# A fixed step order, DMA transposes and casting weight loads for linear attention followed by an MLP

## The chip, the cores and the metric

The kernel runs on one core of one Trainium2 chip. The metric is the device time of one execution in microseconds, as a median of runs. The profile is one execution taken by the hardware profiler; its span is 1.7 to 2.2 us shorter than the time in the runs that have both on record. A run that is over 1.5% above the fastest of its kernel counts as slow; ratios use fast runs alone.

Names of engines in the views: PE is TensorE (matmuls), PEld its weight loads, DVE is VectorE, ACT is ScalarE, POOL is GpSimd, SPq the queue from which the sync engine issues transfers. PEclk is the TensorE clock that was granted, 1.00 being full speed.

## The reference

```python
# q, k, v: (8 batches, 8 heads, 576 tokens, 64), float32
q_s = softmax(q, axis=-1);  k_s = softmax(k, axis=2)          # k over the tokens
kv  = einsum('bhsd,bhse->bhde', k_s, v)
att = einsum('bhsd,bhde->bhse', q_s, kv)
x   = att.transpose(0, 2, 1, 3).reshape(8, 576, 512)
mu, var = mean and variance of x over its 512 columns
xn  = (x - mu) / sqrt(var + 1e-6) * g_ln
out = x + relu(xn @ w_ch1) @ w_ch2                            # 512 x 2048, 2048 x 512
```

There are 8 x 576 = 4608 tokens, that is nine chunks of 512. The MLP takes 128 matmuls of 512 columns for each chunk: 64 `ph` (16 blocks of hidden columns x 4 blocks of input) and 64 `pc` (4 tiles of tokens x 16 blocks of hidden columns), 1152 in all. In both kernels `rstd` is applied after the second matmul, as relu lets it through.

## The kernel before

It is written for a framework whose scheduler orders the instructions of each engine. Chunks of 512 tokens run across batch borders, so the tiles of a batch are cut unevenly. The parts that matter here:

```python
def attn_load(b):                      # per tile of 128 (or 64) tokens
    nc.sync.dma_start(kt[:sz], k[b, :, s0:s0+sz, :].transpose([1, 0, 2]))   # rows of 256 B
    nc.scalar.activation(ek_b[:sz, st], kt[:sz], AF.Exp)
    ...                                # v: load, copy on ScalarE; q: load, exp on ScalarE
    nc.vector.reduce_sum(zq[:sz], eq[:sz], axis=AX.X)
    nc.vector.reciprocal(rq[:sz], zq[:sz])
    nc.vector.tensor_mul(qs_b[:sz, st], eq[:sz], rq[:sz].to_broadcast([sz, H, D]))

def attn_te(b):
    ...                                # pkv: 64 x 65 per head, 5 matmuls each; kv_b = pkv / sum
    nc.tensor.transpose(ptr[:, j, :], qs_b[:, st, 2*j:2*j+2, :], ident)     # q on TensorE
    nc.vector.tensor_copy(out=qsT_b[:, :, s0:s0+sz], in_=ptr[:, :, :sz])
    ...                                # po = qsT x kv_b
    nc.scalar.copy(x_sb[ro:ro+sz, xt, :], po[ro:ro+sz, :])
    nc.vector.bn_stats(stat_all[ro:ro+sz, xt, :], x_sb[ro:ro+sz, xt, :])

def mlp_prep(ci):
    ...                                # bn_aggr
    nc.scalar.activation(lnv, mv[:, :, 1], AF.Ln, bias=eps_ln)      # one table set
    nc.scalar.activation(rstd, lnv, AF.Exp, scale=-0.5)             # another one
    ...
    nc.tensor.transpose(pxt[:, c, :], xn[:, c*P:(c+1)*P], ident)    # xn on TensorE
    nc.vector.tensor_copy(out=xnT[:, :, ti*P:(ti+1)*P], in_=pxt)

def load_w1():                         # 4 pieces through two staging buffers
    nc.sync.dma_start(wt, w1_src[:, ko, :])
    nc.vector.tensor_scalar_mul(w1_sb[:, ko, :], in0=wt, scalar1=g_sb[:, ko:ko+1])

for b in range(1, B):
    mlp_prep(b - 1)
    if b + 1 < B: attn_load(b + 1)
    attn_te(b)
    mlp_mm(b - 1)
```

The softmax here doesn't subtract the row's maximum and nothing guards it: scores larger than these inputs give would overflow.

## Time and profile before

| | before |
|---|---|
| time, median of 3 runs | 372.78 us (370.8 to 373.81) |
| span of the profiled run | 369.5 us |
| TensorE, VectorE, ScalarE busy | 307.5, 180.3, 184.4 us |
| mean granted TensorE clock | 0.968 |

The page gives busy times, slices and the chain of work that ended last; the prediction below shows those lines and reads them. One more passage of the chain, in order of time (start, length, what), shows what a stall in the middle looks like:

```profile
203.53 0.62 ACT eq L137
204.15 0.49 ACT hT L247
...
204.66 1.28 ACT L218
...
206.27 1.28 ACT L219
...
207.77 0.52 ACT ek_ab L128
208.28 0.49 ACT hT L247
...
208.82 1.03 PE ph L237 x4
```

`L218` and `L219` without a tile are loads of activation tables: `Ln` and `Exp` lie in different sets, so ScalarE changes tables twice in each chunk. The relu `hT` stands behind them, and TensorE, with two PSUM buffers for `ph`, stands behind the relu.

### The profile page before, as it was taken

How to read it: one execution, taken by the hardware profiler on the slowest of the kernel's cores; microseconds unless marked ns; L12 is line 12 of the kernel's file. 1: busy time of each engine (PE TensorE's matmuls, PEld its weight loads, DVE VectorE, ACT ScalarE, POOL GpSimd, SP SyncE). 2: the span in 40 equal slices, each digit the busy share in tenths (PEclk: the TensorE clock that was granted, in tenths of full speed). 3: DMA queues.
4: the chain of work that ended last, by engine and by line, in shares of the span. 5: the costliest groups of instructions: out<-in, count | busy, mean ns of one | idle time of the engine just before them, and what ended most of it. 6: DMA issues, size and time to landing. Idle time of an engine off the chain costs nothing.

```text
span 369.5 us, 4982 instructions
## 1 busy us (share of the span) xinstructions
PE 307.5 (83%) x1904; PEld 152.3 (41%) x1936; DVE 180.3 (49%) x403; ACT 184.4 (50%) x321; POOL 0.7 (0%) x6
## 2 busy tenths in 40 slices
PE   0254795889999879997999799879987989997995
PEld 0142243435444534463455345534443443443442
DVE  4577346855584864694459336921370131122021
ACT  4553485635795498178628853672066104402600
POOL 0000000000000000000000000000000000000000
PEclk9999697799999999999999899999999998999999
DMA  9967992799099497399289618500100020011002
GB/s 179 204 242 261 200 254 113 219 240 228 11 224 245 122 227 123 92 220 215 59 205 209 101 36 219 117 2 25 60 30 1 29 86 0 2 57 57 0 30 85
DMA packets 120984, 46.46 MB, mean 126 GB/s; under 512 B 113793, under 2 KB 113793, under 8 KB 120449
## 3 DMA queue, kind: packets, MB, share of 16 engines
q1 hardware_dynamic: 120960, 46.15, 56.7%
q8 instruction: 15, 0.25, 0.3%
q14 instruction: 9, 0.07, 0.1%
HBM read 36.70 MB, written 9.44 MB: 125 GB/s over the span
## 4 chain that ended last, share of the span: by engine, by line
PE 67%; DVE 13%; ACT 9%; DMA 5%; SPq 3%; issue 2%; ACTq 0%; DVEq 0%
PE pc L253 32%; PE ph L237 29%; DMA qt<-in_q_dram 3%; DVE xnT L228 2%; ACT hT L247 2%; ACT x_sb L200 2%; PE ptr L180 2%; DMA wt<-in_moe_w_ch_dram 2%; ACT L219 2%; DVE stat_all L201 2%; DVE zq L139 2%; PE pkv L159 2%; DVE ot L261 2%; PE po L193 1%; SPq L131 1%
## 5 line engine op out<-in xcount | busy, mean ns | idle before, releaser
L237 PE MATMUL ph<-xnT,w_sb 128*128 128x512 bf16 x556 | 139.4, 393 | 18.3 <-ACT hT L247 11.3
L253 PE MATMUL pc<-w_sb,hT 128*128 128x512 bf16 x564 | 129.1, 382 | 2.7 <-DVE w_sb L117 1.8
L247 ACT ACTIVATE hT<-ph 128x512 bf16<-128x512 f32 x126 | 74.4, 597 | 82.4 <-PE ph L237 81.7
L237 PEld LDWEIGHTS <-w_sb 128*128 128x128 bf16 x576 | 56.0, 100 | 84.5 <-issue 26.6
L253 PEld LDWEIGHTS <-hT 128*128 128x128 bf16 x576 | 56.6, 98 | 69.8 <-issue 3.7
L261 DVE SCALAR_TENSOR_TENSOR ot<-pc,rstd,x_sb 128x512 f32<-128x512 f32 x36 | 26.9, 746 | 58.2 <-PE pc L253 58.1
L245 DVE TENSOR_SCALAR hT<-ph 128x512 bf16<-128x512 f32 x18 | 12.4, 688 | 64.8 <-PE ph L237 64.8
L139 DVE TENSOR_REDUCE zq<-eq 128x8 f32<-128x512 bf16 (+1 forms) x40 | 27.1, 677 | 29.1 <-ACT eq L137 29.1
L128 ACT ACTIVATE ek_ab<-kt 128x512 bf16<-128x512 f32 (+1 forms) x40 | 25.1, 626 | 23.5 <-DMA kt<-in_k_dram 23.5
L200 ACT CAST x_sb<-po 128x512 bf16<-128x512 f32 (+1 forms) x40 | 21.8, 588 | 29.3 <-PE po L193 28.8
L132 ACT CAST v_ab<-vt 128x512 bf16<-128x512 f32 (+1 forms) x40 | 24.8, 621 | 19.8 <-DMA vt<-in_v_dram 19.8
L137 ACT ACTIVATE eq<-qt 128x512 bf16<-128x512 f32 (+1 forms) x40 | 25.2, 631 | 8.8 <-DMA qt<-in_q_dram 8.8
L180 PE MATMUL ptr<-ident,qs_ab 128*128 128x128 bf16 x160 | 16.7, 234 | 14.8 <-DVE qs_ab L142 13.2
L142 DVE TENSOR_TENSOR qs_ab<-eq,rq 128x512 bf16<-128x512 bf16 (+1 forms) x40 | 27.4, 686 | 0.9
L201 DVE BATCH_NORM_STATS2 stat_all<-x_sb 128x6 f32<-128x512 bf16 (+1 forms) x40 | 25.5, 679 | 1.8 <-ACT x_sb L200 1.6
L180 PEld LDWEIGHTS <-qs_ab 128*128 128x128 bf16 x160 | 11.9, 104 | 23.2 <-DVE qs_ab L142 17.7
L227 PE MATMUL pxt<-ident,xn 128*128 128x128 bf16 x144 | 13.0, 230 | 10.1 <-DVE xn L224 10.1
L193 PE MATMUL po<-kv_ab,qsT_ab 128*128 128x128 bf16 (+1 forms) x160 | 16.0, 242 | 6.1 <-DVE kv_ab L172 3.6
L185 DVE COPY qsT_ab<-ptr 128x512 bf16<-128x512 bf16 (+1 forms) x40 | 15.1, 392 | 9.8 <-PE ptr L180 9.3
L228 DVE COPY xnT<-pxt 128x512 bf16<-128x512 bf16 x36 | 13.8, 414 | 11.0 <-PE pxt L227 10.8
L159 PE MATMUL pkv<-v_ab,ek_ab 128*64 128x65 bf16 x320 | 11.4, 209 | 6.3 <-ACT v_ab L132 5.9
L193 PEld LDWEIGHTS <-qsT_ab 128*128 128x128 bf16 (+1 forms) x160 | 11.8, 111 | 10.6 <-issue 5.4
(33 smaller groups left out, 89.4 us busy)
## 6 DMA issues: line engine op xcount, KB each, us to landing
out_dram<-ot SPq DMA_DIRECT2D x36, 256.0 KB, 2.1
kt<-in_k_dram SPq DMA_DIRECT2D x32, 256.0 KB, 5.0
vt<-in_v_dram SPq DMA_DIRECT2D x32, 256.0 KB, 5.0
qt<-in_q_dram SPq DMA_DIRECT2D x32, 256.0 KB, 4.8
wt<-in_moe_w_ch_dram SPq DMA_DIRECT2D x4, 1024.0 KB, 6.0
kt<-in_k_dram SPq DMA_DIRECT2D x8, 128.0 KB, 4.8
vt<-in_v_dram SPq DMA_DIRECT2D x8, 128.0 KB, 4.6
qt<-in_q_dram SPq DMA_DIRECT2D x8, 128.0 KB, 4.4
```

What stands on the lines that cost most here:

```text
L128: nc.scalar.activation(ek_b[:sz, st], kt[:sz], AF.Exp)
L137: nc.scalar.activation(eq[:sz], qt[:sz], AF.Exp)
L139: nc.vector.reduce_sum(zq[:sz], eq[:sz], axis=AX.X)
L142: nc.vector.tensor_mul(qs_b[:sz, st], eq[:sz], rq[:sz].to_broadcast([sz, H, D]))
L180: nc.tensor.transpose(ptr[:, j, :], qs_b[:, st, 2 * j : 2 * j + 2, :], ident,)
L193: nc.tensor.matmul(po[ro : ro + sz, j * 128 : j * 128 + 128], qsT_b[:, j, s0 : s0 + sz], kv_b[:, j, :], start=True, stop=True,)
L200: nc.scalar.copy(x_sb[ro : ro + sz, xt, :], po[ro : ro + sz, :])
L201: nc.vector.bn_stats(stat_all[ro : ro + sz, xt, :], x_sb[ro : ro + sz, xt, :])
L237: nc.tensor.matmul(ph, w1_sb[:, ko, m * P : (m + 1) * P], xnT[:, ko, :], start=(ko == 0), stop=(ko == KO1 - 1),)
L247: nc.scalar.activation(hT[:, m, :], ph, AF.Relu)
L253: nc.tensor.matmul(pc, hT[:, ko2, ti * P : (ti + 1) * P], w2_sb[:, ko2, :], start=(ko2 == 0), stop=(ko2 == KO2 - 1),)
L261: nc.vector.scalar_tensor_tensor(ot, in0=pc, scalar=rstd[:, ti : ti + 1], in1=x_sb[:, xt, :], op0=ALU.mult, op1=ALU.add,)
```

## The change

It rewrites nearly the whole kernel with six intentions. The diff below is shortened. The order of all engines is fixed in the source: each chunk is a list of 128 MLP matmuls ("steps"), and the attention of a later batch is put between them at chosen steps. A chunk is the first 512 tokens of one batch; the last 64 tokens of all batches make the ninth chunk. A token's place is chosen so that loads have rows of 1 KB. `eq` and `xn` are transposed by DMA, except for the first two batches. Weights are cast to bf16 by the DMA, from GpSimd's queue. One table set with both functions is loaded once.

```diff
-    def load_w1():
-        for ko in range(KO1):
-            wt = wload.tile([P, DH], FP32, tag="wtmp")
-            nc.sync.dma_start(wt, w1_src[:, ko, :])
-            nc.vector.tensor_scalar_mul(...)
+    def load_w1(nb):
+        nc.gpsimd.dma_start(w1_sb[:, :, cols], w1_src[:, :, cols])   # float32 -> bf16
+    def main_src(x, b, h0, hn):
+        return x[b, h0 : h0 + hn, 0:SM, :].rearrange("h (p t) d -> p h (t d)", t=T)
 ... (kv for two heads at once, 128 x 129) ...
+    def dma_T(dst, src, t0, tn):
+        nc.sync.dma_start_transpose(dst[:, t0:t0+tn].rearrange("p t j c -> p (t j) c"), src)
+    def po_mm(c, t, i):
 ...
+        else:                                  # ninth chunk: two batches in one tile
+            ps = slice(64 * (i // NP), 64 * (i // NP) + 64)
+            nc.tensor.matmul(po[ps, j*P : j*P+P], eqTs[c][:, t, j, ps],
+                             kv_sb[:, 2*t + i // NP, j, :], start=True, stop=True)
+    def x_out(c, t):                           # q's normalisation when po is taken out
+        nc.vector.tensor_mul(x[:, t], pobox["p"], eqs[c][2][:, t].to_broadcast([P, H, D]))
+        stats(c, t, x[:, t])                   # bn_stats, bn_aggr, xn = (x - mean) * g
+    def run(main, side): ...                   # side work at its step between main's matmuls
+    def attn_side(c, kv0, kv1, po0, po1, pe=False):
 ...
+        else:
+            s.append(((po0 + po1) / 2 + 12, lambda: xn_T(c, 0, 2)))
+            s.append((po1 + 12, lambda: xn_T(c, 2, 2)))
+    def first_batch():
+        nc.scalar.preload_act_table_set("natural_log_exp_and_others")
 ...
+        nc.gpsimd.tensor_copy(out=gate, in_=raws[0][0][:, 5, 0, 0:4])   # weights wait for k
+        for nb in range(4): load_w1(nb)
 ...
-    for b in range(1, B):
-        mlp_prep(b - 1) ...
+    with tc.manual_schedule(engines={PE, DVE, Activation, SP, Pool}):
+        first_batch()
+        run(mlp_steps(0), [(60, lambda: load_batch(2))] + prep_side(1, 74, 104, True)
+                          + attn_side(1, 96, 108, 109, 123, True))
+        for c in range(1, B):
+            if c == 1: side += prep_side(2, 0, 30)
+            if c + 1 < B: side += attn_side(c + 1, 34, 54, 62, 90)
+            else:         side += attn_side(C9, 0, 0, 40, 80)
+            if c + 2 < B:
+                side += [(1, lambda b=c + 2: load_batch(b))]
+                side += prep_side(c + 2, 70, 118)
 ...
+            run(mlp_steps(c), side)
+        run(mlp_steps(C9), [])
```

## The prediction

> **What bounds the kernel now.** I read the page first: shares, slices, then the chain of work that ended last.
>
> ```profile
> PE 307.5 (83%) x1904; PEld 152.3 (41%) x1936; DVE 180.3 (49%) x403; ACT 184.4 (50%) x321; POOL 0.7 (0%) x6
> PE   0254795889999879997999799879987989997995
> PEclk9999697799999999999999899999999998999999
> PE 67%; DVE 13%; ACT 9%; DMA 5%; SPq 3%; issue 2%; ACTq 0%; DVEq 0%
> ```
>
> TensorE is the busiest engine and 67% of the chain. But a third of the chain (some 120 us) is other engines, in two places. The first four slices (37 us) hold almost no matmuls. Later most slices are not 9: something interrupts the matmuls in every batch. Next, the groups of instructions, each shape apart:
>
> ```profile
> L237 PE MATMUL ph<-xnT,w_sb 128*128 128x512 bf16 x556 | 139.4, 393 | 18.3 <-ACT hT L247 11.3 <-DVE w_sb L109 3.5 <-DVE xnT L228 1.7
> L253 PE MATMUL pc<-w_sb,hT 128*128 128x512 bf16 x564 | 129.1, 382 | 2.7 <-DVE w_sb L117 1.8 <-issue 0.2
> L180 PE MATMUL ptr<-ident,qs_ab 128*128 128x128 bf16 x160 | 16.7, 234 | 14.8 <-DVE qs_ab L142 13.2 <-DVE xnT L228 1.4
> L227 PE MATMUL pxt<-ident,xn 128*128 128x128 bf16 x144 | 13.0, 230 | 10.1 <-DVE xn L224 10.1
> L201 DVE BATCH_NORM_STATS2 stat_all<-x_sb 128x6 f32<-128x512 bf16 x32 | 20.3, 678 | 0.6 <-ACT x_sb L200 0.5
> L218 ACT ACT_TABLE_LOAD x8 | 10.3, 1283 | 0.1
> ```
>
> The two MLP lines are 1152 matmuls (some records are missing). A mean of 393 ns is a latency of overlapping matmuls, so it can't be multiplied. The pace comes from the chain in order of time, at its start, in one middle batch and in the last chunk:
>
> ```profile
> 31.20 6.91 DMA wt<-in_moe_w_ch_dram
> 39.55 0.62 PE ph L237
> ...
> 135.33 1.28 ACT L219
> 136.83 0.52 ACT ek_ab L128
> 137.89 1.02 PE ph L237 x4
> ...
> 337.88 1.04 PE ph L237 x4
> 352.03 9.28 PE pc L253 x43
> 361.37 4.50 PE pc L253 x20
> 365.88 0.75 DVE ot L261
> ```
>
> The last chunk has no attention beside it and runs from 337.88 to 365.88: 28.0 us for 128 matmuls, 219 ns each. Nine chunks are thus 252 us of the 369.5 us span; I call this the floor, since the change leaves these 1152 matmuls as they are. The other 117 us are about 39 us until matmuls run densely, 3.6 us after the last one, and some 75 us of attention on TensorE and stalls. A stall looks like the middle lines: an activation-table load and an exp sit ahead of the relu that TensorE waits for.
>
> **What the Trainium skill says.** "TensorE: Matmul & The Clock Gate", section "Wait — 56ns, not 53.3ns?", gives 215.7 ns from start to start of warm 512-column matmuls; the trace's 219 ns agrees. "ScalarE: Activation LUTs", section "What ACT_TABLE_LOAD costs", gives 1283 ns for one load; the trace has 1283. Its section "Table sets: the hidden batching unit" has one set with both exp and ln, so one load suffices; the trace shows 17 loads. "DMA: Bandwidth & Descriptors", section "Latency and other measured facts", gives 261 GB/s for a DMA transpose in one kernel. The trace before has no transpose by DMA, so nothing here confirms that; it is the least certain number below.
>
> **The change, part by part.**
>
> *Table loads.* 17 x 1.28 = 21.8 us of ScalarE become one load. Seven or so lie on the chain, about 9 us.
>
> *TensorE beside the MLP.* Before: 304 transposes at 55 ns (the chain shows four in 0.22 us) = 16.7 us; 320 pkv matmuls at 21 ns (36 in 0.76 us) = 6.7; 160 po at about 60 ns = 9.6; sum 33 us. After: 160 kv matmuls of 129 columns at about 55 ns = 8.8; po 9.6; 64 transposes (batches 0 and 1 only) = 3.5; sum 22 us. That saves 11 us. Per later chunk it leaves 20 kv and 16 po, 2.1 us, between the 128 MLP matmuls: 28.0 + 2.1 = about 30 us.
>
> *ScalarE per chunk.* 9 exps x 0.63 + 12 relus x 0.60 + 0.5 = 13.4 us of 30. Copies of v and x leave it. It can't be the bound.
>
> *VectorE per chunk.* The q normalisation moves to the eviction of po: 4 x (0.69 multiply + 0.68 stats + 0.16 aggregate + 0.69 subtract) = 8.9 us; sums and reciprocals of q 3.5; v casts 2; four relus 2.8; outputs 4 x 0.75 = 3.0; kv 1.3; total about 21.5 us of 30. It fits, but the 8.9 us are wanted between steps 62 and 90 of 128, that is 28 x 0.219 + 1 = 7 us. So it runs behind there.
>
> *DMA transposes.* xn of the next chunk goes in two halves of 256 KB, queued at steps 88 and 102, and eq (512 KB) between them. Counted from step 62, VectorE finishes the fourth tile near 1.8 + 8.9 + 0.75 (an output) + 1 (two v casts) = 12.4 us. Step 128 comes at 66 x 0.219 + 1 = 15.4 us. That leaves 3 us for the last half. A 256 KB store lands 2.1 us after its issue in this trace; adding 1 us at the skill's 261 GB/s and 1 us behind eq makes about 4 to 5 us, an estimate. So TensorE waits 1 to 2 us at each of seven boundaries; I take 1.5.
>
> *Start.* Loads have rows of 1 KB in place of 256 B (before: 113793 of 120984 packets are under 512 B, and the first 10 us moved 182 GB/s; the stretch with weight rows of 8 KB moved 282). At some 280 GB/s batch 0 (3.4 MB) is in near 14 us. After that come exp, kv, po, then four tiles of 1.6 us on VectorE and a transpose: the MLP starts near 25 us, not 39. But weights (8.4 MB, cast in the DMA, waiting for most of k) come only then, near 44 us, and batch 1 (3.4 MB) behind them on the same queue, while batch 2 is loaded beside it from step 60. I put batch 1 complete at 60 us (56 to 67). TensorE's order is fixed, so at step 92 of chunk 0 it stands until batch 1 is there. Then come q exps 2.5, k exps 3.2, kv and its scaling 1.5, VectorE's 8.9 and a transpose 1: about 17 us. Chunk 1 starts near 77 us.
>
> *Sum.* 77 + 7 x 30 + 1 (the ninth chunk's 16 extra po) + 28 + 3.6 = 320 us, less 3 for overlap of its tail pieces with the last matmuls and the 1% that 216 ns would save, plus 7 x 1.5 = 10.5 of boundaries, is about 327 us of span. The median time lies 3 us above the profiled span (372.78 against 369.5), so 330; I settle on **328 us**, 12% below the time before.
>
> **The rivals.**
>
> *The transposes become the new wait.* For it: a transfer with a fixed latency stands just before the point where every matmul of the next chunk needs it, and stores and eq share its queue. Against it: the loads of the chunk are issued at step 1, so their 3.4 MB take 12 us and are gone by step 60. At 5 us a boundary instead of 1.5 the time is about 352 us; at 10 us, as if a transpose ran at a fifth of the quoted rate, about 387, slower than before. With 261 GB/s stated, I give that one in twenty.
>
> *The start eats the gain.* The fixed order puts batch 1's attention in chunk 0's queue while weights and two batches share the DMA engines. If casting halves the rate, weights end near 58 us and chunk 1 starts near 92: about 343 us. For it: slices 1 to 14 before show DMA engines mostly at 7 to 9 tenths. Against it: wider rows.
>
> *Nothing stands in the way.* If the DMA runs at 350 GB/s and the transposes fit, chunk 1 starts near 68 us and boundaries cost nothing: about 310 us.
>
> *VectorE becomes the bound.* 21.5 of 30 us speak against it, except in the stretch named.
>
> **Range and chances.** 310 (the best rival) to 350 us (boundaries at 5 us, or a slow start with boundaries of 2 to 3 us). Both bad together make 365, just at the 2% line (372.78 x 0.98 = 365.3). Faster by over 2%: 0.94. Within 2%: 0.03. Slower: 0.03.
>
> **What would show it.** Right: no table load but one; TensorE at 9 tenths from about slice 10 to the end; chunks 30 to 32 us apart; the first dense matmuls near 25 us, a hole of 5 to 15 us between 40 and 75 us that ends on batch 1's load or its exps; at chunk boundaries a wait of 1 to 2 us by ph on the transposed xn. Wrong: boundary waits over 4 us or none; chunk spacing over 33 us with VectorE named; DMA rates under 250 GB/s in the first 50 us; a granted clock below 0.9 after the start, through repeated waits. What I know least are the DMA transpose's latency and the rate of the casting load, since neither is in the trace.

## The result, and the profile after

The time is 345.63 us (345.23 to 347.24, 4 runs) against 372.9 us of the kernel before in the same rounds. The ratio is 0.930, with a 95% interval of 0.925 to 0.935. The change is right in direction and lies in the range, but it gave 27 us where 45 had been forecast.

The page after, for the lines that the prediction shows of the page before:

```profile
PE 294.2 (86%) x1517; PEld 139.8 (41%) x1536; DVE 187.4 (55%) x404; ACT 117.3 (34%) x215; POOL 16.3 (5%) x24
...
PE   0245999669897999799979997998899899999994
...
PEclk9999999969999999899989999999899999999998
...
PE 54%; DVE 29%; DMA 10%; issue 3%; ACT 1%; SPq 1%; ACTq 0%; DVEq 0%
```

The transposes in the view of DMA issues (what, queue, kind, count, median us from issue to landing):

```profile
xnT<-xn SPq DMA_TRANSPOSE x14, 3.2
...
eqT<-eq SPq DMA_TRANSPOSE x7, 4.4
```

ScalarE lost 67 us of work and has left the chain. VectorE took its place, with 29%. The PE row still has a 7 every third or fourth slice. The two lines of transposes are new; by their shapes one of `xn` moves 256 KB and one of `eq` 512 KB.

A chunk begins with its first `ph`. The view of windows, cut at those times, gives one line per chunk: length, busy time of PE, PEld, DVE, ACT and POOL with counts, granted clock, DMA share, GB/s. Here are chunks 0, 1, 2, 3 and 7:

```profile
33.20:74.70 41.50, 35.39 (x193) 16.85 (x196) 23.00 (x56) 15.30 (x30) 0.00 (x0) 0.96 0.65 193
74.70:110.30 35.60, 31.64 (x162) 14.87 (x164) 23.56 (x53) 16.86 (x32) 0.00 (x0) 0.95 0.70 163
110.30:142.20 31.90, 29.71 (x162) 14.43 (x163) 20.64 (x47) 12.46 (x23) 0.00 (x0) 1.00 0.65 174
142.20:176.00 33.80, 31.41 (x162) 14.97 (x165) 20.81 (x47) 12.56 (x23) 0.00 (x0) 0.95 0.83 195
...
274.20:310.80 36.60, 36.26 (x158) 15.11 (x160) 14.82 (x25) 7.67 (x14) 0.00 (x0) 1.00 0.18 51
```

The lengths of chunks 0 to 8 are 41.5, 35.6, 31.9, 33.8, 33.6, 32.1, 32.5, 36.6 and (with the tail) 32.8 us. Three things stand out against the 31.5 us forecast for a middle chunk. Some chunks have 31.9 and some 33.8 us with the same work, at clocks of 1.00 and 0.95. Chunk 1 has 35.6. Chunk 7 has 36.6 us with TensorE busy all the time.

The chain at the boundary of chunks 2 and 3 shows where the boundary's wait comes from:

```profile
136.58 0.75 DVE xn L248
137.33 0.33 DVE vr L147
137.66 0.34 DVE vm L138
138.00 0.66 DVE ot L302
138.66 0.34 DVE vm L138
139.00 0.05 SPq L307
139.05 0.06 issue
139.11 3.08 DMA xnT<-xn
...
142.24 4.88 PE ph L286 x14
```

The fourth `xn` is ready at 137.33, but its transpose starts at 139.11. In between VectorE makes the output tile `ot`, and the sync queue issues something at L307, the store of that tile. The transpose is behind that store on the same queue. TensorE's last `pc` had started at 139.79 and its next matmul starts 2.46 us later, at 142.24; the usual pace is 0.22.

Right after such a wait the clock may halve. The same view of windows for 3.4 us after this boundary, and for the next 3.4 us:

```profile
142.90:146.30 3.40, 3.40 (x10) 1.24 (x9) 0.59 (x4) 1.19 (x2) 0.00 (x0) 0.54 0.27 92
146.40:149.80 3.40, 3.40 (x17) 1.54 (x16) 0.69 (x1) 1.68 (x3) 0.00 (x0) 0.98 1.06 361
```

TensorE is "busy" in both, but only 8 matmuls start in the first and 16 in the second (the counts in the view take in those already running). A stretch of half clock costs half its 3.4 us, 1.7 us. It followed three of the six boundary waits in this run: those before chunks 3, 4 and 6. Why those three and not the others is worked out under "Which gaps halve the clock" below.

### The profile page after: what moved, and what is told of

Its sections match the earlier page's. It is cut to its first block, busy times and chain, and to the rows that moved or that the text cites. A ratio compares the mean times of both kernels' runs of the same rounds, so it can differ in the third digit from the quotient of the medians.

```text
span 343.6 us, 3978 instructions
## 1 busy us (share of the span) xinstructions
PE 294.2 (86%) x1517; PEld 139.8 (41%) x1536; DVE 187.4 (55%) x404; ACT 117.3 (34%) x215; POOL 16.3 (5%) x24
## 4 chain that ended last, share of the span: by engine, by line
PE 54%; DVE 29%; DMA 10%; issue 3%; ACT 1%; SPq 1%; ACTq 0%; DVEq 0%
PE ph L286 38%; PE pc L296 12%; DVE st L246 6%; DMA xnT<-xn 5%; DVE xn L248 5%; DVE x L256 5%; DVE ot L302 3%; DMA eqT<-eq 3%; PE pkv L201 2%; DVE vm L138 2%; DVE mv L247 2%; PE po L239 2%; DMA kt<-in_k_dram 2%; DVE zq L176 1%; DVE eq L428 1%
## 5 line engine op out<-in xcount | busy, mean ns | idle before, releaser
L302 DVE SCALAR_TENSOR_TENSOR ot<-pc,rstd,x 128x512 f32<-128x512 f32 x36 | 26.4, 734 | 20.0 <-PE pc L296 20.0
L233 PE MATMUL po<-kv_sb,eqT 128*128 128x128 bf16 x128 | 26.9, 230 | 4.8 <-DVE kv_sb L210 1.7
L176 DVE TENSOR_REDUCE zq<-eq 128x8 f32<-128x512 bf16 x36 | 23.8, 661 | 10.3 <-ACT eq L164 10.3
L201 PE MATMUL pkv<-vm,ek 128*128 128x129 bf16 x128 | 26.3, 231 | 2.3 <-DVE vm L138 2.3
L248 DVE SCALAR_TENSOR_TENSOR xn<-x,mv,g_bc 128x512 bf16<-128x512 bf16 x36 | 27.1, 752 | 1.3
L256 DVE TENSOR_TENSOR x<-po,rq 128x512 bf16<-128x512 f32 x32 | 21.9, 686 | 7.3 <-PE po L239 5.3
L246 DVE BATCH_NORM_STATS2 st<-x 128x6 f32<-128x512 bf16 x32 | 22.2, 695 | 1.1
L164 ACT ACTIVATE eq<-qt 128x512 bf16<-128x512 f32 x32 | 17.6, 619 | 7.6 <-DMA kt<-in_k_dram 7.0
L132 ACT ACTIVATE ek<-kt 128x512 bf16<-128x512 f32 x32 | 17.8, 617 | 0.1
L138 DVE CAST vm<-vt 128x512 bf16<-128x512 f32 x32 | 13.2, 418 | 0.1
```

Of the source, the lines that this page charges most:

```text
L138: nc.vector.tensor_copy(out=vm[:, b % 2, :, j, 0:P].rearrange("p t (h d) -> p h t d", h=2), in_=raws[b][1][:, hs],)
L176: nc.vector.reduce_sum(zq[:, t], eq[:, t], axis=AX.X)
L201: nc.tensor.matmul(pkv[:, j % 2, 0 : P + 1], lhsT, rhs, start=(t == 0), stop=(t == T))
L233: nc.tensor.matmul(po[:, j * P : j * P + P], eqTs[c][:, t, j, :], kv_sb[:, c, j, :], start=True, stop=True,)
L246: nc.vector.bn_stats(st[:, t], src)
L248: nc.vector.scalar_tensor_tensor(xn[:, t], in0=x[:, t], scalar=mv[:, t, 0:1], in1=g_bc, op0=ALU.subtract, op1=ALU.mult,)
```

## The experiments

Twelve kernels, each beside runs of the kernel before on the same chip; all gave correct results. Ratios are to the kernel before, whose medians were 371.7 to 372.1 us. One run in `auto` and two of the kernel before were slow and are left out of the ratios.

| label | what | median us | ratio, 95% interval |
|---|---|---|---|
| (the change) | | 345.63 | 0.930 (0.925 to 0.935) |
| xn_first | transposed xn ahead of the store | 330.15 | 0.890 (0.886 to 0.893) |
| c9_full | ninth chunk's po with 128 columns | 341.99 | 0.921 (0.917 to 0.925) |
| c9_group | ninth chunk's po in groups of eight | 338.42 | 0.912 (0.907 to 0.916) |
| load_late | batch 3's loads after the eq transpose | 344.87 | 0.929 (0.924 to 0.934) |
| pe_all | no transposes by DMA | 338.63 | 0.913 (0.909 to 0.917) |
| auto | order left to the scheduler | 345.98 | 0.932 (0.927 to 0.936) |
| c0_relief | batch 1 earlier, VectorE relieved | 345.13 | 0.932 (0.925 to 0.940) |
| before_table | before + one table set | 356.93 | 0.961 (0.957 to 0.966) |
| before_cast | before_table + casting loads | 367.58 | 0.989 (0.981 to 0.997) |
| before_cast_gate | the same, loads held back | 357.15 | 0.962 (0.955 to 0.968) |
| three | xn_first + c9_group + load_late | 321.36 | 0.864 (0.860 to 0.868) |
| five | three + VectorE relieved at the start | 318.76 | 0.857 (0.853 to 0.862) |

### xn_first: the order on one queue

```diff
-            s.append((po1 + 12, lambda: xn_T(c, 2, 2)))
+            s.append((po1 + 4.5, lambda: xn_T(c, 2, 2)))
```

In the two traces TensorE, ScalarE and GpSimd carry out the same instructions in the same order; on the sync queue the transpose stands one store earlier.

> Only the order on the sync queue changes: the second half of the transposed xn is queued ahead of the store of the second output tile. Theory A (the queue's order: the transpose stands behind a store that waits for an output tile on VectorE, 1.76 us from the end of the last xn at 137.33 to the start of the transpose at 139.11): each of the boundary gaps of chunks 2 to 6, 2.5 to 2.7 us between matmuls, falls to 0.7 to 1.0 us; 5 to 6 gaps x 1.7 = 8.5 to 10 us faster, and up to 3 x 1.7 = 5 us more if the stretches of half clock after gaps go too: 330 to 337 us. Theory B (the transfer itself is the wait: the 256 KB transpose queues behind the 512 KB one): the gaps stay at 2.5 us and the time at 345 us. Theory C (VectorE is too late whatever the queue does): no change either, but the transpose starts within 0.2 us of the last xn in the trace.

The time fell by 15 us, at the far end of theory A. The sync queue of this kernel at the boundary of chunks 2 and 3:

```profile
134.50 1.23 SPq L180 DMA_TRANSPOSE xnT<-xn  x1
135.82 0.53 SPq L307 DMA_DIRECT2D out_dram<-ot  x1
```

The view of windows of the same kernel, for chunks 2 and 3:

```profile
107.50:137.60 30.10, 29.69 (x162) 14.43 (x164) 20.81 (x48) 12.46 (x23) 0.00 (x0) 1.00 0.69 184
137.60:167.70 30.10, 29.72 (x162) 14.58 (x165) 20.58 (x46) 12.67 (x23) 0.00 (x0) 1.00 0.92 218
```

The fourth `xn` ends at 134.47 in this run, so the transpose now starts 0.03 us behind it, and the store follows. Chunks 2 to 5 last 30.1 us each, the 30 us of the prediction's sum. The gaps at these boundaries fell from 2.5 to 2.7 us to 0.65 to 0.69 us from start to start, and no half clock follows. The span fell by 16.1 us (343.6 to 327.5): the six gaps are shorter by 10.1 us together, and three half-clock stretches of 1.7 us are gone. Theories B and C fall: the transfer was not slow and VectorE was not too late. There is no slack, though: at the boundary shown the transpose lands at 137.56, TensorE's next matmul starts at 137.60, and without the wait it would have started at 137.14.

### c9_full and c9_group: the ninth chunk's po

In chunk 7 each of the 32 `po` with 64 columns of weights sits alone between MLP matmuls. The timeline of the changed kernel, and of c9_group (start, us from the first start to the last end, count):

```profile
283.67 0.24 PE L239 MATMUL po<-kv_sb,eqT 128*64 128x128 bf16 x1
283.85 0.39 PE L286 MATMUL ph<-xnT,w_sb 128*128 128x512 bf16 x1
284.17 0.24 PE L239 MATMUL po<-kv_sb,eqT 128*64 128x128 bf16 x1
```

```profile
283.68 0.42 PE L239 MATMUL po<-kv_sb,eqT 128*64 128x128 bf16 x8
284.04 2.33 PE L286 MATMUL ph<-xnT,w_sb 128*128 128x512 bf16 x10
```

From `po` to `po` it is 0.50 us with one `ph` of 0.22 between, so a lone `po` costs 0.28 us. Between 128-column `kv` matmuls in other chunks the same distance is 0.27 us, and a small matmul costs 0.055. In c9_group eight in a row take 0.36 us from the first one to the next `ph`.

```diff
 c9_full:
-            po[ps, j*P : j*P+P], eqTs[c][:, t, j, ps], kv_sb[:, 2*t + i//NP, j, :]
+            po[:, j*P : j*P+P],  eqTs[c][:, t, j, :],  kv_sb[:, 2*t + i//NP, j, :]
             # second PSUM tile from i == 4 on; x takes rows 0-63 of one, 64-127 of the other
 c9_group:
-        s += [(po0, lambda: start_x(c))] + spread(fns, po0, po1)
+        s += [(po0 + (po1 - po0) * t / T, f) for t in range(T) for f in fns[t*n : t*n+n]]
```

> The 32 po matmuls of the ninth chunk use all 128 columns of weights, each half of the rows taken from its own PSUM tile; four more VectorE multiplies of 0.7 us. Theory A (TensorE pays about 0.22 us at each change between a 128-column and a 64-column set of weights): a po in chunk 7 costs 0.055 us instead of 0.28, chunk 7 lasts about 30 us instead of 36.6, the whole 6 to 7 us faster, near 339 us. Theory B (the po of this chunk is slow because it alternates between the kv of two batches or waits for its transposed eq): chunk 7 stays at 36 us and the time at 345 us.

> The 32 po matmuls of the ninth chunk keep their 64 columns, but the eight of a tile run back to back, so there are 4 groups in place of 32 places. Theory A (a cost per change of the column group): 4 groups x (2 or 3 changes) x 0.22 us = 2 to 3 us in place of 7, so 4 to 5 us faster, near 341 us. Theory B (a cost per 64-column matmul itself): no change, 345 us.

Chunk 7 fell from 36.6 to 32.1 us with full columns, where three gaps of 0.8 to 1.4 us before `po`, two of them waits for a PSUM tile of over 1 us, ate a part; the whole fell by 3.6 us, less than the 6 to 7 expected. In groups it fell to 29.5 us, and the whole by 7 us, more than the 4 to 5 expected. Since c9_group keeps all 32 matmuls with 64 columns and c9_full keeps all 32 places and the alternation between two batches, the cost is that of changing between the two forms, not of either form. The Trainium skill, "TensorEngine Tiling (Array Packing)", section "Key Properties", says that changing the tiling mode drains TensorE. That the cost is this drain no run shows by itself; its size is in the lines above: the step from `ph` to `po` takes 0.32 us in place of 0.22 and the step back 0.18 in place of 0.055, about 0.22 us for both.

### load_late: a transpose among loads

```diff
-                side += [(1, lambda b=c + 2: load_batch(b))]
+                side += [(20 if c == 1 else 1, lambda b=c + 2: load_batch(b))]
```

> Batch 3's loads move from step 1 to step 20 of chunk 1, behind the transpose of batch 2's eq. Theory A (the transpose shares the DMA engines with 3.4 MB of loads): its time from issue to landing falls from 9.7 us to about 4.5 us, the gap of 2.0 us at 90.5 us goes, and the time falls by 1.5 to 2 us, to 344 us. Theory B (the transpose itself takes that long, or waits for the exps): it stays above 8 us and nothing changes. Risk: the loads then meet batch 3's exps at step 70, which would put the gap later.

The longest of the seven `eq` transposes fell from 9.7 to 5.4 us from issue to landing, and the gap at 90.8 us went. Chunk 1 fell from 35.6 to 33.8 us. So theory A holds for the place. The whole gained only 0.8 us, within the noise. Half of chunk 1's gain was lost before it: this run started chunk 1 at 75.6 us instead of 74.7, and kernels with the same chunk 0 start it anywhere from 74.0 to 76.2. In `three`, below, chunk 1 gains 1.7 us against xn_first.

### pe_all: no transposes by DMA

```diff
-                side += prep_side(c + 2, 70, 118)
+                side += prep_side(c + 2, 70, 118, True)      # and all other uses: pe=True
-                (po0 + (po1 - po0) * (t + 2.5) / T, lambda t=t: xn_pT(c, t, nc.scalar))
+                (po0 + (22, 34, 47, 59)[t], ...)             # when VectorE has the tile
```

> Every transpose by DMA is undone: eq and xn of all chunks are transposed on TensorE and copied by ScalarE, which is busy 34% of the time. Theory A (the transposes by DMA cost time only by the boundary waits): 224 more transposes x 0.055 = 12.3 us more on TensorE and ScalarE 56 x 0.59 more, against 6 boundary gaps of 2.3 us and one eq gap of 2 us saved: within 6 us of the changed kernel, 340 to 352 us. Rival (moving transposes off TensorE is a large part of the gain): over 355 us.

It is 7 us faster than the change, a little below the range of theory A. Chunks 2 to 6 last 31.4 us each, with no gap over 0.9 us: 1.3 us above those of xn_first, for 32 transposes. So transposes by DMA are worth 1.3 us a chunk when they are queued in time, and as the change queues them they lose more than that.

### auto: the order left to the scheduler

```diff
-    with tc.manual_schedule(engines={...}):
+    if True:
```

> The same program, with the order of the engines' instructions left to the scheduler, as in the kernel before. Theory A (the fixed order is what fills TensorE): attention and MLP are no longer interleaved by steps, stalls of several us come back in each chunk, 355 to 385 us. Rival (the smaller work and the wider loads give the gain, not the order): 340 to 350 us.

345.98 us, the same as with the fixed order: the rival is right about the time. The chunks show that it isn't the same kernel. Chunks 0, 1 and 3:

```profile
31.50:89.50 58.00, 38.74 (x216) 18.76 (x219) 29.18 (x81) 26.01 (x50) 0.69 (x1) 0.87 1.04 259
89.50:126.10 36.60, 32.85 (x160) 15.06 (x161) 26.41 (x71) 13.86 (x26) 0.00 (x0) 0.92 1.01 267
...
156.20:186.00 29.80, 29.69 (x163) 14.43 (x163) 20.12 (x45) 12.22 (x23) 0.00 (x0) 1.00 0.26 63
```

The scheduler needs 16.5 us more for chunk 0, where it puts batch 2's loads early; VectorE then waits for loads, once for 12.5 us, TensorE stands for 10.9 and 4.0 us, and the clock is granted at 0.87. But its middle chunks last 29.7 us: it fills TensorE as well as any order of steps, and it queues the transposes in time. The fixed order gained some 16 us in chunk 0 and gave them back at its own boundaries and half-clock stretches. With one line moved (xn_first) it is 16 us better than the scheduler.

### before_table: one part alone, the table set

```diff
+    nc.scalar.preload_act_table_set("natural_log_exp_and_others")
     attn_load(0)
```

> The kernel before with one table set that holds both exp and ln, loaded once; nothing else is changed. Theory A: of the 17 loads x 1.28 us some seven lie on the chain that ended last, so 6 to 10 us faster, 363 to 367 us. Rival (their time is hidden, or taken up by the next wait for ScalarE): less than 2 us, 371 us.

15 us faster, well beyond theory A's 6 to 10. The same place in the chain as the stall shown before:

```profile
197.05 0.53 ACT ek_ab L128
197.58 0.47 ACT x_sb L200
198.05 0.51 ACT hT L247
...
198.60 3.74 PE ph L237 x16
```

The two loads have gone from between the exps and the relu, and matmuls run on behind it. The kernel before also had half-clock stretches at 209.7 us, right after this stall, and at 305.3 us; neither is there now, 1.7 us each. So this one line gives 3.9% alone on the old kernel, where the whole change gives 7.0%. What it is worth inside the change no run shows.

### before_cast and before_cast_gate: one part alone, casting loads

```diff
-            nc.sync.dma_start(wt, w1_src[:, ko, :])
-            nc.vector.tensor_scalar_mul(w1_sb[:, ko, :], in0=wt, scalar1=g_sb[:, ko:ko+1])
+            nc.gpsimd.dma_start(w1_sb[:, ko, :], w1_src[:, ko, :])     # w2 alike; g goes into xn
 before_cast_gate, besides:
+            if b == 0 and st == 3:                 # the load overwrites it, so it waits for k
+                nc.gpsimd.tensor_copy(out=w1_sb[:, ko, 0:4], in_=kt[:, 0, 0:4])
```

> The kernel before with one table set (357 us) and, besides, weights cast in the DMA from the GpSimd queue, with g in the xn instruction. Theory (the two staging buffers and VectorE's 10 us of casts hold up the first chunk, whose matmuls run densely only from 39.5 us): dense matmuls from about 34 us, 3 to 6 us faster, 351 to 354 us. Rival (hidden: the first chunk's attention or the loads set it, and the xn instruction, 0.75 us in place of 0.34, costs 36 x 0.41 = 15 us of VectorE): 356 to 362 us.

> The kernel before with one table set and weights cast in the DMA, which alone came to 367.6 us with dense matmuls only from about 57 us. Here the two weight loads wait, as in the changed kernel, until a late k tile of batch 0 (w1) or of batch 1 (w2) is in. Theory (the weights, asked for at 1 us, shared the DMA engines with batch 0's loads and put its last q off from 17 to 39 us): dense matmuls from 36 to 42 us and 350 to 358 us, at or below the 356.9 us with staged casts. Rival (the casting load or the longer xn instruction is the cost): 363 us or more.

Without the gate it lost 11 us against before_table: neither forecast held, and it is slower than even the rival's 356 to 362. The sync queue shows the weights, which GpSimd asked for in the first microseconds, in the way of batch 0's loads:

```profile
2.58 10.04 SPq L119 DMA_DIRECT2D kt<-in_k_dram  x1
12.67 6.47 SPq L123 DMA_DIRECT2D vt<-in_v_dram  x1
19.18 6.47 SPq L127 DMA_DIRECT2D qt<-in_q_dram  x1
```

In the kernel before, issuing the same `kt` load took 1.06 us, and the q of the fourth tile landed at 17.3 us instead of 39.1. The Trainium skill, "DMA: Bandwidth & Descriptors", section "Issuing engines are not separate DMA queues", says that transfers from all queues run on the same engines and interleave; this is that, in numbers. With the gate the time is 357.15 us, against 356.93 with staged casts: the cast in the DMA, together with the longer xn instruction that comes with it, is worth nothing in the old kernel, and the gate keeps it from costing 3% there. The two parts were not separated.

### c0_relief: VectorE's chain in chunk 0

```diff
+        if b == 1: nc.scalar.copy(dst, raws[b][1][:, hs])        # v casts; eq copies alike
-            + prep_side(1, 74, 104, True) + attn_side(1, 96, 108, 109, 123, True)
+            + prep_side(1, 66, 86, True)  + attn_side(1, 84, 96, 97, 118, True)
```

> In chunk 0, batch 1's attention starts 8 to 12 steps earlier and its v casts and eq copies move from VectorE (the chain from 55 to 74 us) to ScalarE, idle there. Batch 1's q exps ran at 48.9 us, so its data were in. Theory A (chunk 1 starts late because VectorE's 20 us of work start late and are too much, not because of the loads): chunk 1 starts at 69 to 71 us instead of 74.5; 3.5 to 5.5 us faster, 340 to 342 us. Rival, the prediction's own (batch 1's loads set it): chunk 1 still starts near 74 us and the time stays at 345 us.

Chunk 1 started at 72.7 instead of 74.7 us, short of theory A's 69 to 71. Chunk 1 then lasted 37.7 instead of 35.6: `po` waited 4.4 us in place of 2.0 for the same `eq` transpose among batch 3's loads. The gain was turned into a longer wait for the DMA, and the time stayed. Theory A has the place right but not the gain, and the rival as stated (batch 1's loads) wasn't what held it.

### three and five: the repairs together

`three` takes the edits of xn_first, c9_group and load_late. `five` adds c0_relief's edits, for batch 0 too, with k exps and v casts of batch 0 ahead on ScalarE and v's loads on the sync queue.

> The changed kernel with three repairs: transposed xn ahead of the store, ninth chunk's po in groups, batch 3's loads behind the transpose. If their gains belong to different places in the span they add: 330.2 - 7.2 - 1.8 = 321 us. If the half-clock stretches, which differ from run to run, had been part of single gains: 320 to 325 us. Rival (a gap removed in one place is waited for in the next): 327 us or more.

> The three repairs and two reliefs of VectorE by ScalarE: batch 1's attention earlier with v casts and eq copies on ScalarE (alone it moved chunk 1 from 74.5 to 72.5 us, and the eq transpose behind batch 3's loads took it back), and the same for batch 0, with its v loads on the sync queue, so that ScalarE, which issued loads until 9.0 us, can start its exps when q is in. Theory (VectorE's chain of some 20 us from 11 to 33 us sets the start): the MLP starts at 28 to 30 us in place of 33.2, chunk 1 at 68 to 70 us, the whole 314 to 317 us. Rival (weights or batch 1's loads set it): the MLP starts early but waits for weights, or chunk 1 still starts near 74 us: 320 us.

`three` came to 321.36 us where 321 was the sum of two single gains and of the 1.8 us expected of load_late: they belong to different places and add. In `five` the MLP starts at 27.8 us in place of 33.2, close to the 28 to 30 expected, but chunk 1 still starts at 73.7, not at 68 to 70, and the time misses the 314 to 317 us: the rival held. The chain shows what holds it:

```profile
13.73 8.99 DMA w_sb<-in_moe_w_ch_dram
...
23.00 24.50 DMA qt<-in_q_dram
...
47.52 0.63 ACT eq L165
```

Batch 1's q, queued behind the weights, lands at 47.5 us, near the 48.9 at which the change began its q exps, so an earlier start is spent before it: TensorE stands for 2.2 us until 48.2, and chunk 0 runs at a granted clock of 0.87, at half clock up to 32.8 and from 49.9 to 56.7 us. The gain over `three`, 2.6 us, is 1.3 us of an earlier chunk 1 and 1.4 of a shorter one (30.4 us for 31.8). `five` is the fastest version here, 14.3% below the kernel before and 7.9% below the change (0.857 over 0.930).

## Why the prediction was right or wrong

**Where the time lies.** Measured less forecast, with 31.5 us forecast for a chunk: start and chunk 0 -2.3 us, chunk 1 +4.1, chunks 2 to 6 +6.4, chunk 7 (32.5 with its extra po) +4.1, chunk 8 and the tail +1.2, and 3.0 us of overlap that were taken off. Together they are the 16.5 us by which the span of 343.6 us missed the sum of 327.1.

**Direction and bound: right.** TensorE stays the bound; the last chunk's MLP takes 27.8 us against the 28.0 before; a middle chunk without waits takes 30.1 us (xn_first) for the 30 of the sum. A small matmul costs 0.055 us if it has the form of its neighbours.

**VectorE at the boundary: right.** The prediction put 10.6 us (12.4 less 1.8) from the first eviction of `po` to the fourth `xn`; it took 10.75 us, from 126.58 to 137.33.

**The boundary wait: right in kind, mis-sized, with a wrong reason.** The term was 1.5 us, with "1 us behind eq". Five gaps were 2.5 to 2.7 us and a sixth 1.35, of which 0.2 is the usual pace; the seventh boundary had none. The transpose did not wait behind eq; it waited 1.78 us behind a store on the same queue, and the store for VectorE. From issue to landing it took 3.1 us, so the 4 to 5 us of the sum came true with another cause. That was to be read in the diff: step 102 lies behind step 95, where the store is emitted. Nor did the term hold the clock, which took 1.7 us more after three of the boundaries, although the clock row before already showed 6 and 7 tenths in slices 5, 7 and 8. Waits (13.0 us) and stretches (5.1) are 18 us, against 10.5 in the sum; xn_first takes 15 of them away.

**The ninth chunk's po: a step that failed.** "1 (the ninth chunk's 16 extra po)" took every small matmul at 0.06 us. With 64 columns, alone between wide ones, each cost 0.28: 32 x 0.28 = 9.0 us, some 7 more than allowed; in c9_group chunk 7 is 7.1 us shorter.

**The start: sum nearly right, parts wrong.** The MLP was to start at 25 us and started at 33.2. The sum left out that VectorE normalises q (4 x 1.55 us) before it can turn to kv; `five`, which relieves it, starts at 27.8. Batch 1 was to be complete at 60 us, and its q exps ran at 48.9. The two errors nearly cancelled, which is luck: chunk 1 started at 74.7 for 77. The hole forecast on batch 1's load was not there; TensorE stood in gaps of 1.0 to 1.6 us from 61 us on, mostly behind VectorE.

**Chunk 1: a missing term.** 35.6 us for 31.5. Batch 2's exps and transpose fall into this chunk, and the transpose took 9.7 us among loads. The prediction treated loads only as gone by step 60, which holds from chunk 2 on.

**Table loads: seen, but a gain too small.** "About 9 us" was the share of the loads on the chain; alone they were worth 15 us. The chain counts the loads' own time and not the slower clock after a stall: by the granted clocks (0.968 of 369.5 us, 0.981 of 355.5) the kernel before lost 11.8 us to it and before_table 6.8. That is an estimate, from one profile each; 9 and 5 us make 14 of the 15.

**The last step of the sum** took off 3 us for overlaps and 2 more when settling. No view stood behind either, and without them the estimate had been 333 us. The 3 us from span to time set a median of runs against one profile; in the runs that have both on record it is 1.7 to 2.2.

**Rivals.** "The transposes become the new wait" is what happened, through the queue's order rather than the transfer's rate. "The start eats the gain" did not: the chunks after it did. The silent premise that the fixed order is what fills TensorE fell with `auto`.

**Which gaps halve the clock.** In the changed kernel the stretches began at 71.5, 143.2, 177.3 and 242.1 us, whose distances (71.7, 34.1, 64.9) are 21, 10 and 19 times 3.41 us. That fits a clock decided at fixed intervals, as the Trainium skill, "TensorE: Matmul & The Clock Gate", section "What's actually happening", describes: a window of 3413 ns that runs freely. Cut into these intervals, the trace tells the gaps apart. Those before chunks 3, 4 and 6 lie whole in one interval, in which TensorE was idle (no matmul running, by the trace) for 2.08, 2.18 and 2.30 us, and the next interval is at half clock. Those before chunks 2 and 5 fall across the edge of two (0.95 and 1.33 us, 0.46 and 1.63), and the clock stays. The 14 traces have 1185 intervals at full clock. After the 1129 with less than 1.75 us of idle time the clock never fell, after the 31 with more than 2.03 us it always did, and of the 25 between 11 were followed by half clock. So a repair need not remove a gap; here it was enough to make it short. No run set out to test this.

What stays open: how much of the change's other 3% comes from which of its parts. The wider loads, the chunks of one batch and the third PSUM buffer for `ph` were not tried alone.

## What to carry to other kernels

Where a transfer feeds the next stage, read the whole queue in order, and put it ahead of stores that wait for something later: one line was worth 4.4% here. Before a rewrite, try each of its cheap parts alone on the old kernel, since saving the table loads that way gave more than half as much as this whole change. Keep matmuls of one form together, and give loads a start that does not meet those needed first.

## What the Trainium skill lacked or had wrong

- "DMA: Bandwidth & Descriptors", section "Latency and other measured facts", gives a transpose's rate but no time from issue to landing. Here 256 KB took 3.2 us and 512 KB 4.4 us in the median: 256 KB more for 1.2 us, an estimate of 218 GB/s (the page has 261 for one kernel). It is a rough one, since six of the seven larger ones are issued while a smaller one is still under way. Beside 3.4 MB of loads 512 KB took 9.7 us.
- "TensorE: Matmul & The Clock Gate", section "Why this matters for your kernels", warns of idle gaps over about 3 us. Here gaps of 2.46 to 2.68 us from start to start were followed by 3.4 us of half clock in three of five cases, 1.7 us each: about 2 us of idle time within one interval of 3.41 us was enough.
- "TensorE: Matmul & The Clock Gate", section "Part 4: PE-mode transpose", gives about 275 ns in a kernel and 390 ns alone for one 128 x 128 transpose. In the kernel before one lasts 230 to 234 ns in the mean, and in a row they start 55 ns apart (four in 0.22 us), which that section doesn't say.
- "TensorEngine Tiling (Array Packing)" says that a change of mode drains TensorE, without a size. A 64-column matmul alone between 128-column ones cost 0.28 us instead of 0.055; eight in a row took 0.36 us until the next wide one.
- "ScalarE: Activation LUTs", section "What ACT_TABLE_LOAD costs", prices the load itself rightly at 1283 ns, but a switch with its drain at 2.66 us; in the chain before, the second load starts 0.33 us after the end of the first, with `lnv` (0.30 us) between them, so no such drain shows. No page joins the stall behind a load with TensorE's clock: 17 loads cost 15 us in all, by the run without 16 of them.
